# Attention, gated mixing and spatial gating on one core: how the probability-times-value products are queued, when the last weight chunks are read, and how fast the mixing is fed in

## The chip, the cores and the metric

The kernel runs on one core of one Trainium2 chip. The metric is the device time of one execution in microseconds. Three runs of the kernel before took 533.68, 536.41 and 536.85 us; the median, 536.41 us, is the time before. The engines are named as the profile names them: PE (TensorE, with PEld for its weight loads), DVE (VectorE), ACT (ScalarE), POOL (GpSimd), and SP, which issues most DMAs. Each engine works through its own list of instructions in order.

## The reference, cut to what matters

```python
# attention: B=4 batches, H=8 heads, S=576 positions, D=64
scores = q @ k.T / 8 + min(-(cum[:, None] - cum[None, :]), 0)   # causal, cum = cumsum(max(s, 0))
attn   = exp(scores - rowmax) / (rowsum + 1e-9)
x      = (attn @ v), heads side by side -> (B, 576, 512)
# gated mixing, then a spatial gate
gate = sigmoid(causal 5-tap convolution of x with conv_w)
y    = (gate * (x @ w_val)) @ w_out
h    = relu(y @ w_in);  u, v = halves of h
v_n  = (v - mean) / sqrt(var + 1e-6)
out  = (u * (w_spatial @ v_n + b_spatial)) @ w_out2
```

All of it is in fp32; where the kernel multiplies matrices of the mixing it splits each operand in a high and a low part and adds three products (`three`, L398 to L406).

## The kernel before, in words

The program is a Python function that emits instructions; a scheduler, which steps a model of the engines, then decides the order in which each engine's list holds them. What it is given is the order of emission, the dependencies, priorities, and here and there an order rule (`tc.issue_after(i)`: what is emitted inside the block stands behind instruction i). Nothing is looked at on the chip to choose the order: the lists are fixed.

**Attention, head by head.** The main loop (L674 to L713) steps over w = 0 to 32. At step w it computes the scores of head w in five query tiles (`scores`, L185): the scores' matmuls (L204 for the first eight heads, L206 and L207 after), a DVE reduction with the mask that gives the row's maximum (L214), and on ACT the exponential with its row sum (L219). It also transposes the probabilities of head w-1, 15 blocks of 128x128 in four banks, on PE (L266), and ACT copies each bank from PSUM to the tile `pt` (L267). Every second step it treats the finished pair of heads w-2 and w-1: the row sums are transposed on PE (`psr`, L234), copied by ACT (L236), written to DRAM by a DMA from ACT's queue (`r_d`, L237), and read back spread over the partitions by two DMAs from SP's queue (`R`, L243).

**The pair's products.** `pv` (L271) multiplies the transposed probabilities with v: 12 fp32 products for a pair, each of which is two MATMUL instructions on the chip. Head j = 0 writes PSUM partitions 0 to 63, head j = 1 partitions 64 to 127, so the two use the two halves of PE's columns. One group writes `psq` (the first 128 query positions: one 128-wide product per head), the other writes `pso` (the other 448 positions: widths 448, 448, 320, 192 and 64 per head). DVE then multiplies by `R` into the tile x (L289), and `conv` (L294) begins the convolution on ACT (L298) and goes on with four DVE steps (L301). In emission order each product is its own instruction with its own dependencies, so the scheduler may place each wherever the model has room. The first product of head j = 0 needs only that head's probabilities, which are there one step before those of head j = 1.

**Mixing, fed in between.** The mixing of a batch (`mixing_a`, L490, and `mixing_b`, L512) is a generator that yields after each group of 8 to 14 matmuls the time that the group is worth (1.44, 1.68 or 2.56). It is fed in five times per step by `more` (L606): a step adds `n_g` to an account, and groups are emitted until it is used up. `n_g` is 3 up to step 8, then 11.5, 10.0, 9.0 (steps 17 to 24) and 9.5 (steps 25 to 32). One batch is about 60 of these units. Batch b is queued at step 8(b+1)+1, the last batch behind the loop. The mixing's groups are what PE does while an attention step waits for ACT and DVE.

**The end.** Behind the loop (L714 to L718) `load_ahead` (L474) issues reads of weight chunks (512 KB each) for the third batch (`wo_d`) and the last batch (`wv_d`) into tiles that come free: `wv`, `pt`, `qk`, `cn`, `kd`. Then the last batch's `mixing_a` and `mixing_b` are emitted. `mixing_a` begins with xvh and xvl (L72, L79), the split of the four x tiles; its first matmuls (L404 to L406) need all four x tiles, so also the last pair's.

Of the kernel before, what the change touches and what calls it, by code (L numbers as in the profile page):

```python
# [24 lines left out]
def tile_stickbreak_attention_moe(  # L25
# [18 lines left out]
    NH, S = s.shape  # L44
    B = out.shape[0]
    H = NH // B
# [11 lines left out]
    BLK, w = {}, 0  # L58
# [5 lines left out]
    V, G, A, T, SY = nc.vector, nc.gpsimd, nc.scalar, nc.tensor, nc.sync  # L64
# [45 lines left out]
    cn = [early.tile([128, S], F32R, name=f"cn{i}") for i in range(2)]  # L110
    kds = [early.tile([128, S], F32R, name=f"kd{i}") for i in range(2)]
# [16 lines left out]
    r_d = dram.tile([NH // 2, 2, 5, 128], F32, name="r_d")  # L128
    wv_d = dram.tile([NP, 128, 2, 512], F32, name="wv_d")
    wo_d = dram.tile([NP, 128, 2, 512], F32, name="wo_d")  # L130
# [47 lines left out]
    LAST = {}  # L178
# [43 lines left out]
    R = {}  # L222
# [16 lines left out]
    def spread_sums(p):  # L239

        R[p] = early.tile([128, 5, 128], F32, tag="R", name="R", bufs=2)
        for j in range(2):
            SY.dma_start(R[p][64 * j:64 * j + 64].rearrange("p i q -> p (i q)"),  # L243
                         r_d[p, j].rearrange("i q -> (i q)").partition_broadcast(64))

    def evac_split(dst_hi, dst_lo, src):
        A.activation(dst_hi, src, AF.Copy)
# [23 lines left out]
    def pv(h):  # L271

        b, p = h // H, (h % H) // 2
        x = X[b, p] = early.tile([128, S], F32, tag=f"x{p}", name=f"x{p}", bufs=1)
        r = R.pop(h // 2).rearrange("p i q -> p (i q)")
        pts = [PT.pop(h + j) for j in range(2)]
        vs = [vraw.pop(h + j) for j in range(2)]
        for tag, q0, q1 in (("q", 0, 128), ("o", 128, S)):
            po = ps.tile([128, 512], F32, tag=tag, name=f"ps{tag}", bufs=1)
            cs = [c for c in range(5) if c * 128 < q1 and (c == 0 or q0 > 0)]  # L280
            for c in cs:
                a = max(q0, c * 128)
                o = BLK[c, c] + a - c * 128
                for j in range(2):
                    T.matmul(po[64 * j:64 * j + 64, a - q0:q1 - q0], vs[j][:, c, :], pts[j][:, o:o + q1 - a],  # L285
                             start=c == 0, stop=c == cs[-1])
            for a, e in ((q0, 64), (64, q1)) if q0 == 0 else ((q0, q1),):
                o = a + 64 if a else 0
                V.tensor_tensor(out=x[:, a:e], in0=po[:, a - q0:e - q0], in1=r[:, o:o + e - a], op=ALU.mult)  # L289
# [118 lines left out]
    KC = list(range(NP))  # L408
# [62 lines left out]
        key = src is wo_d, b, mc  # L471
        return AHEAD.pop(key) if key in AHEAD else load_chunk(src, mc)

    def load_ahead(src, b, homes):  # L474

        for mc, home in zip(KC, homes):
            AHEAD[src is wo_d, b, mc] = load_chunk(src, mc, home)

    def gated_split(dh, dl, psrc, other):
# [135 lines left out]
    def first_steps():  # L615
        nonlocal cw
        cw = early.tile([128, NP, 5], F32, name="cw")
        V.tensor_copy(cw, from_f64(conv_w, 20).rearrange("p (c k) -> p c k", k=5))
        order = [(lambda mc=mc: weight_prep(w_val, wv_d, mc)) for mc in KC]
        order += [(lambda mc=mc: fold_prep(mc, None)) for mc in KC]  # L620
        order = order[4:] + order[:4]
        for o in order:
            o()
            yield
        for kc in KC:
            fold_prep(kc, 1)
            yield
        for ec in range(4):
            fold(ec, 1)
            yield 2.56  # L630
# [14 lines left out]
    first = first_steps()  # L645
# [27 lines left out]
    for w in range(NH + 1):  # L673
        if w == H + 1:  # L674
            queue.clear()
            queue.append(start())
        elif w % H == 1 and w > 1 and w < NH:
            queue += [mixing_a(w // H - 1), mixing_b(w // H - 1)]
        if w >= NATIVE:
            load(w + 2)  # L680
        n_g = [3, 11.5, 10.0, 9.0, 9.5][0 if w <= H else 1 if w <= H + 4 else 2 if w <= 2 * H else 3 if w <= 3 * H else 4]
        gs = [n_g / 5] * 5
        if w < NH:
            scores(w, [0, 1])
        if w > 0:
            transposes(w - 1, [1, 2])
        if w % 2 == 0 and w > 0:
            lay_sums(w // 2 - 1)
        more(gs[0])
        if w < NH:  # L690
            scores(w, [2])
        prep(w + 1)
        if w > 0:
            transposes(w - 1, [3])
        more(gs[1])
        if w < NH:
            scores(w, [3])
        if w > 0:
            transposes(w - 1, [0])
        if w % 2 == 0 and w > 0:  # L700
            spread_sums(w // 2 - 1)
        more(gs[2])
        if w < NH:
            scores(w, [4])
            if w < NATIVE:
                load(w + 2)
            if w % 2:
                normalise(w // 2)
        more(gs[3])
        if w % 2 == 0 and w > 0:  # L710
            pv(w - 2)
            conv((w - 2) // H, ((w - 2) % H) // 2)
        more(gs[4])  # L713
    load_ahead(wo_d, B - 2, ["wv", "wv", "pt", "pt"])  # L714
    load_ahead(wv_d, B - 1, ["qk", "qk", cn, kds])
    queue += [mixing_a(B - 1), mixing_b(B - 1)]
    while queue:
        more(1)  # L718
# [50 lines left out]
```

## Time and profile before

| what | before |
|---|---|
| median of 3 runs | 536.41 us |
| profiled execution, its own time | 538.75 us |
| its span (first to last instruction) | 537.0 us |
| PE busy | 503.1 us, 94% of the span |
| ACT busy | 342.9 us, 64% |
| DVE busy | 314.0 us, 58% |
| POOL busy | 126.1 us, 23% |
| moved by DMA | 71.36 MB, mean 133 GB/s |
| mean granted TensorE clock | 0.981 |

The profile is one execution. In its views "busy" is the time in which an engine had an instruction, "x" the number of instructions, PEclk the granted clock of PE as a share of full speed (1.00 is the 2.4 GHz level, 0.50 the 1.2 GHz level). In a timeline, rows are instructions in order of time; equal neighbours are merged, and a bracket at the end is the idle time of the engine before the row with what ended it. Matmuls overlap: the duration of one is longer than the distance to the start of the next, so what a run of matmuls costs PE is read from start to start.

### The profile page before, as it was taken

What the parts mean: (1) busy time and instruction counts of PE and PEld (TensorE: products, weight loads), DVE (VectorE), ACT (ScalarE), POOL (GpSimd) and SP (SyncE); (2) the same over time, 40 slices, a digit from 0 to 9 for tenths busy, and PEclk for the clock granted to TensorE, in tenths of its full rate; (3) what the DMA queues carried; (4) which work ended last, traced back from release to release, by engine and by line L of the source; (5) the groups of instructions that cost most, each with busy time, mean ns of one, the idle gap of its engine ahead of it and who ended that gap; (6) DMA issues with size and microseconds to landing.
All of it is one profiled execution on the core that took longest, in us unless ns stands there. A gap on an engine that the chain in (4) does not pass through costs nothing.

```text
span 537.0 us, 9116 instructions
## 1 busy us (share of the span) xinstructions
PE 503.1 (94%) x3206; PEld 417.2 (78%) x3206; DVE 314.0 (58%) x836; ACT 342.9 (64%) x821; POOL 126.1 (23%) x166
## 2 busy tenths in 40 slices
PE   8777988999989999999999999999999999299997
PEld 4344655788768898988889898888789987298997
DVE  5778589788988865624886464565545541325120
ACT  3897679798678764954666475684867655234322
POOL 5220130016450112203351120032501300135240
PEclk9999889999999999999999999999999999689999
DMA  6949655437662633285331305763030178500002
GB/s 186 282 130 260 189 180 156 153 100 260 198 228 77 193 94 106 80 256 179 115 94 56 105 10 166 233 200 118 13 95 12 37 212 271 179 0 2 1 0 89
DMA packets 28910, 71.36 MB, mean 133 GB/s; under 512 B 4096, under 2 KB 12448, under 8 KB 28864
## 3 DMA queue, kind: packets, MB, share of 16 engines
q1 hardware_dynamic: 23936, 65.98, 40.6%
q10 hardware_dynamic: 4928, 4.80, 2.7%
q8 instruction: 25, 0.41, 0.3%
q14 instruction: 21, 0.17, 0.1%
HBM read 58.06 MB, written 9.16 MB: 125 GB/s over the span
## 4 chain that ended last, share of the span: by engine, by line
PE 64%; ACT 13%; DMA 12%; DVE 7%; issue 3%; SPq 1%; ACTq 0%; POOL 0%; DVEq 0%
PE psm L404 11%; PE psm L406 10%; PE psm L405 10%; PE pso L285 7%; PE pst L266 6%; PE psm L576 3%; PE psm L577 3%; PE psm L578 3%; ACT p L219 3%; DMA wg<-in_w_in 3%; PE pss L206 3%; DMA wr<-in_w_out 2%; PE pss L207 2%; ACT pt L267 2%; DMA R<-r_d 2%
## 5 line engine op out<-in xcount | busy, mean ns | idle before, releaser
L219 ACT ACTIVATE p<-p,nm 64x64 f32<-64x64 f32 (+4 forms) x160 | 88.6, 555 | 10.5 <-DVE nm L214 10.2
L266 PE MATMUL pst<-ident,p 128*128 128x128 f32 x480 | 77.6, 276 | 7.4 <-ACT pt L267 4.6
L214 DVE CUSTOM_DVE_ANT_0 p<-pss,mask 64x64 f32<-64x64 f32 (+4 forms) x160 | 64.3, 419 | 30.3 <-PE pss L207 19.2
L267 ACT ACTIVATE pt<-pst 128x512 f32<-128x512 f32 (+1 forms) x128 | 61.9, 494 | 21.8 <-PE pst L266 13.1
L266 PEld LDWEIGHTS pst<-ident,p 128*128 128x128 f32 x480 | 57.0, 141 | 22.8 <-ACT pt L267 8.2
L285 PE MATMUL pso<-pt,vraw 128*64 128x448 f32 (+3 forms) x320 | 66.1, 438 | 2.0 <-ACT pt L267 2.0
L301 DVE SCALAR_TENSOR_TENSOR z<-x,cw,z 128x575 f32<-128x575 f32 (+1 forms) x64 | 55.5, 867 | 6.9 <-ACT z L298 6.4
L79 POOL TENSOR_TENSOR g<-gt,g 128x288 fp32r<-128x288 f32 x32 | 28.5, 898 | 126.5 <-ACT g L72 126.5
L79 POOL TENSOR_TENSOR y<-gt,y 128x288 fp32r<-128x288 f32 x32 | 27.1, 845 | 108.9 <-ACT y L72 108.8
L206 PE MATMUL pss<-qk 128*64 128x64 f32 (+1 forms) x144 | 45.6, 333 | 1.1 <-DVE nm L214 1.1
L285 PEld LDWEIGHTS pso<-pt,vraw 128*64 128x64 f32 x320 | 28.4, 140 | 18.3 <-issue 8.7
L207 PE MATMUL pss<-kd,cn 66*64 66x64 f32 (+1 forms) x144 | 41.9, 296 | 0.0
L404 PE MATMUL psm<-g,wch 128*128 128x288 f32 x128 | 39.1, 306 | 0.0
L576 PE MATMUL psm<-wsh,vh 128*128 128x288 f32 x128 | 38.5, 303 | 0.0
L405 PE MATMUL psm<-g,wcl 128*128 128x288 f32 x128 | 37.8, 296 | 0.0
L406 PE MATMUL psm<-g,wch 128*128 128x288 f32 x128 | 37.7, 296 | 0.0
L577 PE MATMUL psm<-wsh,vl 128*128 128x288 f32 x128 | 37.5, 295 | 0.0
L578 PE MATMUL psm<-wsl,vh 128*128 128x288 f32 x128 | 37.5, 295 | 0.0
L404 PE MATMUL psm<-y,wv 128*128 128x288 f32 x112 | 34.3, 306 | 0.6 <-ACT pt L267 0.4
L481 DVE TENSOR_TENSOR gt<-psm,u 128x288 f32<-128x288 f32 x32 | 14.5, 454 | 34.7 <-PE psm L580 24.2
L406 PE MATMUL psm<-y,wv 128*128 128x288 f32 x112 | 33.1, 297 | 0.0
L405 PE MATMUL psm<-y,wv 128*128 128x288 f32 x112 | 32.9, 295 | 0.0
(171 smaller groups left out, 1310.9 us busy)
## 6 DMA issues: line engine op xcount, KB each, us to landing
raw<-in_qk SPq DMA_DIRECT2D x24, 576.0 KB
wv<-wo_d SPq DMA_DIRECT2D x16, 512.0 KB
wv<-wv_d SPq DMA_DIRECT2D x12, 512.0 KB
vraw<-in_vp SPq DMA_DIRECT2D x32, 160.0 KB
R<-r_d SPq DMA_DIRECT2D x32, 160.0 KB
out<-ot ACTq DMA_DIRECT2D x32, 144.0 KB
cn<-qk SPq DMA_DIRECT2D x24, 144.0 KB
wr<-in_w_in SPq DMA_DIRECT2D x5, 512.0 KB
```

The lines of the kernel that those rows point to most:

```text
L79: eng.tensor_tensor(out=out_, in0=in_, in1=f(hi), op=ALU.subtract)
L206: T.matmul(pst[0:m, o:o + b - a], qa[:, q0:q0 + m], kb[:, a:b], start=True, stop=False)
L214: LAST["V"] = V.tensor_tensor_reduce(out=p[i][0:m, a:b], in0=src, in1=mask[0:m, o:o + b - a], scale=-0.125, scalar=3.0e38 if a == 0 else n ...
L219: A.activation(p[i][0:m, 0:e], p[i][0:m, 0:e], AF.Exp, bias=nm[0:m, i:i + 1], scale=-1.0, accum_out=sm[h // 2 % 2][0:m, h % 2, i:i + 1])
L266: T.transpose(pt[:, o - o0:o - o0 + 128], p[i][:, c * 128:(c + 1) * 128], ident[:, r:r + 128])
L267: A.activation(PT[h][:, o0:end], pt[:, 0:end - o0], AF.Copy)
L285: T.matmul(po[64 * j:64 * j + 64, a - q0:q1 - q0], vs[j][:, c, :], pts[j][:, o:o + q1 - a], start=c == 0, stop=c == cs[-1])
L301: V.scalar_tensor_tensor(out=z[:, d:], in0=x[:, :S - d], scalar=cw[:, p, k:k + 1], in1=z[:, d:], op0=ALU.mult, op1=ALU.add)
L404: T.matmul(pt, ah, bh, start=j == 0, stop=False)
L405: T.matmul(pt, al, bh, start=False, stop=False)
L406: T.matmul(pt, ah, bl, start=False, stop=j == n - 1)
L576: T.matmul(o, vh[c][:, cs], wsh[:, c, hs[hf]], start=c == 0, stop=False)
```

## The change

Three edits:

1. In `pv` the pso group comes before the psq group, its first product is now that of block c = 1 of head j = 1, which reads the last bank that `transposes` fills, and every other product of the pair is emitted under `issue_after(first)`.
2. Behind the loop, only the first two `wo_d` chunks are issued freely. The other two and the four `wv_d` chunks are emitted under `issue_after` of the last `R` read.
3. `n_g` is 7.6 instead of 9.0 for steps 17 to 24 and 6.0 instead of 9.5 for steps 25 to 32.

```diff
-            SY.dma_start(R[p][64 * j:64 * j + 64].rearrange("p i q -> p (i q)"),
-                         r_d[p, j].rearrange("i q -> (i q)").partition_broadcast(64))
+            LAST["R"] = SY.dma_start(R[p][64 * j:64 * j + 64].rearrange("p i q -> p (i q)"),
+                                     r_d[p, j].rearrange("i q -> (i q)").partition_broadcast(64))
...
-        for tag, q0, q1 in (("q", 0, 128), ("o", 128, S)):
+
+        first = None
+        for tag, q0, q1 in (("o", 128, S), ("q", 0, 128)):
             po = ps.tile([128, 512], F32, tag=tag, name=f"ps{tag}", bufs=1)
-            cs = [c for c in range(5) if c * 128 < q1 and (c == 0 or q0 > 0)]
+            cs = [1, 0, 2, 3, 4] if q0 else [0]
             for c in cs:
                 a = max(q0, c * 128)
                 o = BLK[c, c] + a - c * 128
-                for j in range(2):
-                    T.matmul(po[64 * j:64 * j + 64, a - q0:q1 - q0], vs[j][:, c, :], pts[j][:, o:o + q1 - a],
-                             start=c == 0, stop=c == cs[-1])
+                for j in (1, 0):
+                    with ExitStack() as es:
+                        if first is not None:
+                            es.enter_context(tc.issue_after(first))
+                        m = T.matmul(po[64 * j:64 * j + 64, a - q0:q1 - q0], vs[j][:, c, :], pts[j][:, o:o + q1 - a],
+                                     start=c == cs[0], stop=c == cs[-1])
+                    first = first or m.ins
...
-    def load_ahead(src, b, homes):
+    def load_ahead(src, b, homes, mcs=KC):
-        for mc, home in zip(KC, homes):
+        for mc, home in zip(mcs, homes):
...
-        n_g = [3, 11.5, 10.0, 9.0, 9.5][0 if w <= H else 1 if w <= H + 4 else 2 if w <= 2 * H else 3 if w <= 3 * H else 4]
+        n_g = [3, 11.5, 10.0, 7.6, 6.0][0 if w <= H else 1 if w <= H + 4 else 2 if w <= 2 * H else 3 if w <= 3 * H else 4]
...
-    load_ahead(wo_d, B - 2, ["wv", "wv", "pt", "pt"])
-    load_ahead(wv_d, B - 1, ["qk", "qk", cn, kds])
+    load_ahead(wo_d, B - 2, ["wv", "wv"])
+    with tc.issue_after(LAST["R"].ins):
+        load_ahead(wo_d, B - 2, ["pt", "pt"], KC[2:])
+        load_ahead(wv_d, B - 1, ["qk", "qk", cn, kds])
```

What this does to the order shows best at three places. The first is PE's list around the eighth pair of heads, of 16. In the kernel before, its products stand in four pieces; here are the rows of the pieces with the row next to each (L207 is a scores matmul, L404, L576 and L580 are mixing matmuls, L266 a transposition; "x2" are two products of the same form):

```order
730 L207 MATMUL pss<-kd_99,cn_97 128x288
731 L285 MATMUL pso<-pt,vraw 64x448
732 L404 MATMUL psm<-g,wch 128x288
...
840 L285 MATMUL psq<-pt,vraw 64x128 x2
841 L285 MATMUL pso<-pt,vraw 64x448 x2
842 L266 MATMUL pst<-ident,p_106 128x128
...
870 L580 MATMUL psm<-ws_1735,s_137 128x288
871 L285 MATMUL pso<-pt,vraw 64x448
872 L285 MATMUL pso<-pt,vraw 64x320 x2
873 L285 MATMUL pso<-pt,vraw 64x192 x2
874 L285 MATMUL pso<-pt,vraw 64x64 x2
```

The same pair in PE's list of the changed kernel:

```order
824 L207 MATMUL pss<-kd_98,cn_96 128x288
825 L290 MATMUL pso<-pt,vraw 64x448 x4
826 L290 MATMUL pso<-pt,vraw 64x320 x2
827 L290 MATMUL pso<-pt,vraw 64x192 x2
828 L290 MATMUL pso<-pt,vraw 64x64 x2
829 L290 MATMUL psq<-pt,vraw 64x128 x2
830 L206 MATMUL pss<-qk 64x64
```

All 12 products now stand in one piece, head beside head, where before the first stood alone some 110 rows ahead. Of the 16 pairs, nine stand in one piece in the changed list; the second, third and fifth have the two psq products in a piece of their own; the ninth and the tenth have the last psq product alone, some 20 rows behind; the sixth is in three pieces; and in the eleventh each of the first four 448-wide products has a mixing matmul between it and the next. Only in the first and the fourteenth pair does the piece follow directly on a transposition.

The second place is SP's list at the end of the loop (R is the read of the spread row sums, the others are weight chunks). Before:

```order
187 L466 DMA wv<-wo_d 128x1024 x3
188 L466 DMA wqk<-wv_d 128x1024
189 L466 DMA wv<-wo_d 128x1024
190 L462 DMA cn_97<-wv_d 128x512
191 L462 DMA kd_99<-wv_d 128x512
192 L466 DMA wv<-wo_d 128x1024 x2
193 L466 DMA wpt<-wo_d 128x1024 x2
194 L243 DMA R<-r_d 64x640 x2
195 L466 DMA wpt<-wo_d 128x1024 x2
```

And in the changed kernel:

```order
186 L243 DMA R<-r_d 64x640 x4
187 L472 DMA wqk<-wv_d 128x1024 x2
188 L468 DMA cn_96<-wv_d 128x512
189 L468 DMA cn_97<-wv_d 128x512
190 L468 DMA kd_98<-wv_d 128x512
191 L468 DMA kd_99<-wv_d 128x512
192 L472 DMA wpt<-wo_d 128x1024 x2
193 L472 DMA wv<-wo_d 128x1024 x2
194 L472 DMA wpt<-wo_d 128x1024 x2
```

The last pair's two reads of R stood behind all but two of the late chunks and now stand ahead of all of these. The changed list also holds four `wo_d` reads fewer (16 instead of 20): before, the third batch's `mixing_b` had already read its own chunks when `load_ahead` read them again.

The third place is PE's list behind the last pair's products. Before, the next rows are the rest of the last batch's first two groups, which read the last pair's x. In the changed list 166 mixing matmuls of the third batch stand between (70 of the spatial stage, L582 to L586, and 96 of the last product, which read y), and only then the last batch begins; this is where it does:

```order
2341 L410 MATMUL psm<-y,wpt 128x288
2342 L411 MATMUL psm<-y,wpt 128x288
2343 L412 MATMUL psm<-y,wpt 128x288
2344 L410 MATMUL psm<-xvh_5150,wqk 128x288
2345 L411 MATMUL psm<-xvh_5150,wqk 128x288
```

Before, 18 of the last batch's matmuls stood ahead of the last pair's products; now none does.

## Rows read from the trace of the kernel before

**Rows 1.** The page, part 1: busy time of each engine
```profile
PE 503.1 (94%) x3206; PEld 417.2 (78%) x3206; DVE 314.0 (58%) x836; ACT 342.9 (64%) x821; POOL 126.1 (23%) x166
```

**Rows 2.** Windows: stretch, its length, busy time per engine, clock, DMA share
```profile
core 0: us, PE busy (x) PEld busy (x) DVE busy (x) ACT busy (x) POOL busy (x), PEclk, DMA share, GB/s
0.00:100.00 100.00, 83.94 (x403) 51.87 (x404) 75.02 (x223) 74.01 (x193) 22.82 (x39) 0.97 0.67 196
100.00:180.00 80.00, 77.55 (x466) 62.16 (x465) 66.85 (x167) 65.78 (x150) 25.05 (x28) 1.00 0.53 165
180.00:445.00 265.00, 263.62 (x1830) 230.68 (x1829) 149.84 (x401) 173.47 (x420) 56.07 (x69) 1.00 0.39 119
445.00:456.00 11.00, 10.26 (x75) 8.13 (x73) 1.38 (x6) 5.43 (x12) 0.00 (x0) 1.00 0.90 313
456.00:465.00 9.00, 0.01 (x1) 0.01 (x1) 1.49 (x4) 1.35 (x2) 0.00 (x0) 0.70 0.85 269
465.00:473.10 8.10, 7.01 (x28) 6.66 (x29) 4.34 (x8) 3.19 (x5) 2.68 (x3) 0.50 0.00 2
```

**Rows 3.** Windows of line L285 alone: length, PE busy, PEld busy, clock, DMA
```profile
0.00:100.00 100.00, 19.75 (x96) 9.10 (x96) 0.97 0.67 196
100.00:180.00 80.00, 10.81 (x58) 4.22 (x58) 1.00 0.53 165
180.00:445.00 265.00, 37.36 (x206) 16.11 (x206) 1.00 0.39 119
```

**Rows 4.** Timeline of PE around the eighth pair: start, duration, line, operation, tiles
```profile
188.24 0.29 PE L207 MATMUL pss<-kd,cn 66*128 66x288 f32 x1
188.46 0.97 PE L285 MATMUL pso<-pt,vraw 128*64 128x448 f32 x2
189.36 0.40 PE L404 MATMUL psm<-g,wch 128*128 128x288 f32 x1
...
203.78 0.44 PE L285 MATMUL psq<-pt,vraw 128*64 128x128 f32 x4
204.05 0.92 PE L285 MATMUL pso<-pt,vraw 128*64 128x448 f32 x4
...
208.90 1.94 PE L285 MATMUL pso<-pt,vraw 128*64 128x448 f32 x14
```

**Rows 5.** Timeline of PE at the last pair and behind it
```profile
446.74 0.30 PE L405 MATMUL psm<-y,wv 128*128 128x288 f32 x1
446.88 0.29 PE L406 MATMUL psm<-y,wv 128*128 128x288 f32 x1
...
452.34 0.97 PE L285 MATMUL pso<-pt,vraw 128*64 128x448 f32 x4
...
453.36 1.89 PE L285 MATMUL pso<-pt,vraw 128*64 128x448 f32 x14
464.99 0.61 PE L404 MATMUL psm<-xvh,wqk 128*128 128x288 f32 x1 [9.74 <-ACT xvh L72]
465.40 0.44 PE L405 MATMUL psm<-xvh,wqk 128*128 128x288 f32 x1
465.64 0.44 PE L404 MATMUL psm<-xvh,wqk 128*128 128x288 f32 x1
...
467.89 0.61 PE L404 MATMUL psm<-xvh,wqk 128*128 128x288 f32 x1 [1.09 <-DVE gt L481]
```

**Rows 6.** The chain that ended last: row sums of two pairs, start and duration
```profile
94.79 1.93 DMA r_d<-rt
...
97.26 3.85 DMA R<-r_d
...
451.52 4.82 DMA r_d<-rt
456.86 5.69 DMA R<-r_d
```

**Rows 7.** The page, part 5: ACT's copies of transposed banks
```profile
L267 ACT ACTIVATE pt<-pst 128x512 f32<-128x512 f32 (+1 forms) x128 | 61.9, 494 | 21.8 <-PE pst L266 13.1
```

## The prediction

> **What bounds the kernel now.** First the page's busy times: PE is busy 503.1 of 537.0 us, no other engine above 64% [rows 1]. A share over the whole span mixes stages, so next the windows [rows 2]. From 180 to 445 us PE is busy 263.62 of 265 us at full clock while ACT is busy 65% and DVE 57%: here PE is the limit, and every microsecond of PE work removed is a microsecond, as long as no wait replaces it. From 0 to 100 us PE is busy 84%, ACT 74%, DVE 75%, and the DMA share is 0.67: a chain through several engines. From 100 to 180 us PE is busy 97%, but DVE 84% and ACT 82%: PE work removed there may surface on the others. Then 456 to 465 us: nothing runs on PE at all, and from 465 to 473.1 us it runs at granted clock 0.50, the 1.2 GHz level, after that idle time.
>
> Two things are to be seen below these totals. In the timeline around a pair [rows 4], the first 448-wide product stands alone: two MATMULs that hold PE from 188.46 to 189.36, 0.90 us. At 452.34 four such MATMULs, one product of each head, take 0.97 us, just what the two take alone (0.97) [rows 4, 5]: the two heads' products run side by side in the two halves of the columns, so a product without its partner wastes half of PE. In the timeline behind the last pair [rows 5], PE waits 9.74 us for the last batch's xvh. The chain says why [rows 6]: the last pair's row sums took 4.82 us to DRAM and 5.69 us back, where an earlier pair's took 1.93 and 3.85; the DMA share was 0.90 and 0.85 around them [rows 2], which is the late chunks.
>
> **The change, part by part**, against the profiled execution's 538.75 us.
>
> *The end.* In the changed order 166 mixing matmuls stand between the last pair's products and the first that needs its x. Warm, one follows the other at 0.134 us (446.74 to 446.88) [rows 5], so they cover 22 us. What they must cover: before, with slow transfers, the wait was 9.74 us. So the gap goes even if the transfers stay slow, and with the chunks behind R they should fall towards 1.93 and 3.85 us. The next wait, 1.09 us at 467.89 for DVE's gating behind the convolution, is under the same cover. The half clock goes with the gap that preceded it: 7.01 busy us at a distance of 0.24 us (465.40 to 465.64) instead of 0.134 [rows 2, 5] cost 7.01 x (1 - 0.134/0.24) = 3.1 us. Together 9.74 + 1.09 + 3.1 = 13.9 us. What is late next are the chunks themselves: two `wo_d` chunks in `pt` are needed 118 matmuls (15.8 us) behind the pair, and 2 MB of `wv_d` plus 1 MB of `wo_d` must land by then or 22 us. At the 313 GB/s of the stretch 445 to 456 us [rows 2], 3 MB take 10 us. They fit, with 6 us to spare; the four repeated reads that are gone make it easier.
>
> *The pairs, 180 to 445 us.* Line L285 is busy 37.36 us for 206 MATMULs [rows 3]; a pair has 24, so this is 8.6 pairs at 4.35 us each. The price of one piece can be read: in the last pair 11 of 12 products stand together, from 452.34 to 453.36 + 1.89 = 455.25, 2.91 us [rows 5], and the twelfth fits beside them, since head 1 with all six of its products is the longer side already. Saved per pair 4.35 - 2.91 = 1.44 us, times 8.6 = 12.4 us; the last pair adds its lone product, 0.90 us (the same form as at 188.46). Against that, three pairs of the changed order are not whole: two have a lone psq product (about 0.45 us each, an estimate: the two 128-wide products at 203.78 hold PE 0.27 us before the next group, and a piece of its own costs an entry and an exit), and the eleventh has four lone 448s, 4 x 0.90 = 3.6 instead of at most 2 x 0.97 us side by side, with its entries 2.0 us more. Net 12.4 + 0.9 - 2.9 = 10.4 us. Each entry into a piece costs PE 0.22 us after a 288-wide matmul instead of 0.134 (188.24 to 188.46) [rows 4]; three fewer per pair would be 2 us more. I leave that out, since busy time counts the overlap of a piece's last MATMUL with the next row, which is about as much.
>
> *The pairs, 0 to 180 us.* From 100 to 180 us 58 MATMULs take 10.81 us [rows 3]: 2.4 pairs at 4.47, so at most 3.8 us. DVE and ACT are over 80% busy there; between nothing and all I take half, 1.9. From 0 to 100 us, four pairs take 19.75 us, waits and half clock included; at most 4 x 1.5 = 6 us. PE is not the limit there; I take a quarter, 1.5.
>
> *The slower feeding.* No work is removed: 1.4 and 3.5 units per step move behind the attention, where PE has nothing else, so this costs nothing by itself and fills the gap above. Its price is cover. In steps 25 to 32 a step loses 3.5 units, 3.9 us of PE's work at 12 matmuls of 0.134 us for 1.44. What may come bare: ACT's convolution start waits for x, x for R, and the exponentials of the next head queue behind it on ACT. With 1.93 + 3.85 us and some 0.5 us of issue [rows 6], R lands 6.3 us behind the row sums' copy. In the changed order these four pairs' products begin 36 to 57 rows behind the row sums' transposition, 5 to 8 us, and take 2.9. So from 0 (R lands first) to 6.3 us for each of four pairs, 25 us. The stretch from 180 to 445 us, where PE idles 1.4 of 265 us with the same chain in it [rows 2], is nearest: I take 2.5 us.
>
> Sum: 538.75 - 13.9 - 10.4 - 1.9 - 1.5 + 2.5 = 513.6. The median of before is 2.3 us below its profiled execution, so 511.2 as the median of runs.
>
> On thinning there is a rule that speaks against it. At 180 to 445 us, with transpositions mixed in, the clock was 1.00; at 0 to 100 us, where feeding is 3 units a step, it was 0.97 [rows 2]. The Trainium skill ("TensorE: Matmul & The Clock Gate", Part 4, PE-mode transpose) states that transposes do not count as PE-busy in the way other matmuls do, so a stage with less mixing could lose the clock. By the trace's rows at 1.00 the sum stays 511.2; by that rule it would be the third rival below.
>
> **The rivals.**
> - *The pairs give nothing*: ACT and DVE or the heads' chain set the steps once PE is faster. For it: 82 to 84% busy before 180 us. Against it: 57 to 65% after, and PE waits of 1.4 us. Only the end is gained: 536.4 - 13.9 = 522.5.
> - *All of it arrives*: no new waits, and the pairs bring 10.4 + 3.8 + 6 = 20.2, since x comes sooner from whole pieces and the steps before 180 us shorten with them: 536.4 - 13.9 - 20.2 = 502.3. Against it: PE's 84% before 100 us.
> - *The thinned stage behaves like the opening*: PE busy 84%, clock 0.97 [rows 2]. A step before took 265 / 17.2 heads = 15.4 us; less 3.9 and half of 1.44 it is 10.8, eight of them 86 us. 16% of that is 14 us of waits, and 3% is 3 us of clock: 511.2 + 17 = 528. Against it: ACT had weights to convert in the opening, and none here.
> - *Slower*: each piece waits at the head of PE's list for ACT to copy the last bank, with everything behind it held. It decides from (25.2 + 5.4)/16 = 1.9 us a pair, the whole gain and 1% more. An ACT copy is 0.49 us [rows 7], so it would take two or three other ACT instructions ahead of it each time. In the changed order only 2 of 16 pieces follow directly on a transposition, so it should stay at a microsecond or two in all; if it held for every pair at 2.5 us, 551 (511.2 + 40).
>
> **How the numbers follow.** Chances: the forecast (505 to 518) 0.62, all of it (about 502) 0.13, nothing from the pairs (about 522) 0.13, the opening's behaviour (about 528) 0.08, slower 0.04. The predicted time is the forecast's, 511. The range 502 to 523 takes in the bounds of the pairs' saving and leaves out the last two cases and half of the second, near 2 in 10. A measurement of this kernel can tell about 1%, so faster is below 531.0: 0.62 + 0.13 + 0.13 and the faster edge of the fourth, 0.89; within 1% 0.07; slower 0.04.
>
> **What would show it.** Right: no PE wait over 2 us before the last batch's first matmul and granted clock 1.00 from 440 us on; L290 at about 3 us per pair; the last r_d and R near 2 and 4 us; 2 MB less moved. Wrong: PE busy below 95% in steps 25 to 32, with DVE's x waiting for R or ACT's z for x ahead of exponentials; a PE wait for `wpt` behind the last pair; a granted clock of 0.50 in that stage; pairs at 3 us with the stage no shorter.

## The result and the profile after

| what | before | after |
|---|---|---|
| median | 536.6 us (4 runs) | 523.4 us (522.2 to 524.2, 4 runs) |
| ratio after/before | | 0.975, interval 0.972 to 0.979 |
| profiled execution, its span | 538.75, 537.0 us | 524.15, 522.4 us |
| moved by DMA | 71.36 MB | 69.27 MB |
| mean granted clock | 0.981 | 0.967 |

The change is a gain of 13.3 us in the medians. The prediction was 511.0 us with a range of 502 to 523, so it had the sign, but the gain came out about half as large: the time lies 0.4 us above the range. That it lies near the rival in which the pairs give nothing (522.5) is chance, as the terms below show.

The page's busy times of after, then its windows by the stretches of [rows 2] (stretch, its length, busy time of each engine, granted clock, DMA share; the end is cut otherwise, since the gap is gone):

```profile
PE 493.0 (94%) x3206; PEld 414.2 (79%) x3206; DVE 316.6 (61%) x836; ACT 339.9 (65%) x819; POOL 125.1 (24%) x166
0.00:100.00 100.00, 86.52 (x406) 54.35 (x408) 78.45 (x227) 76.11 (x195) 22.47 (x39) 0.90 0.64 197
100.00:180.00 80.00, 73.73 (x441) 58.90 (x438) 62.32 (x159) 60.30 (x140) 23.87 (x28) 0.94 0.51 156
180.00:340.00 160.00, 158.05 (x1143) 140.96 (x1143) 101.05 (x265) 107.62 (x269) 33.58 (x40) 1.00 0.42 129
340.00:430.00 90.00, 86.94 (x616) 75.97 (x615) 49.88 (x143) 66.74 (x154) 18.39 (x25) 0.98 0.40 122
430.00:480.00 50.00, 48.69 (x319) 45.32 (x318) 17.98 (x34) 17.01 (x36) 17.31 (x24) 1.00 0.27 85
```

The end is as forecast: 48.69 of 50 us busy at clock 1.00, where before had a hole and half clock [rows 2]. The opening is worse than in [rows 2]: the clock is 0.90 for 0.97 up to 100 us, and from 100 to 180 us PE is busy 73.73 us at 0.94 where it was 77.55 at 1.00. From 180 to 430 us PE now stands still 5.0 of 250 us, before 1.4 of 265.

The windows of the pair products' line, now L290 (length, PE busy, PEld busy, clock), and the timeline of PE at the eighth and the eleventh pair (start, duration, line, tiles, equal neighbours merged):

```profile
180.00:430.00 250.00, 32.44 (x240) 15.18 (x240) 0.99 0.41 126
...
205.94 2.70 PE L290 MATMUL pso<-pt,vraw 128*64 128x448 f32 x20
208.47 0.39 PE L290 MATMUL psq<-pt,vraw 128*64 128x128 f32 x4
...
296.36 0.96 PE L290 MATMUL pso<-pt,vraw 128*64 128x448 f32 x2
297.26 0.40 PE L412 MATMUL psm<-g,wch 128*128 128x288 f32 x1
297.59 0.96 PE L290 MATMUL pso<-pt,vraw 128*64 128x448 f32 x2
298.48 0.40 PE L410 MATMUL psm<-g,wch 128*128 128x288 f32 x1
```

A whole pair takes 2.92 us (205.94 to 208.86), where the prediction had 2.91, and ten pairs take 3.24 each for 4.35 in [rows 3]. The eleventh, and in part three others, are not whole: mixing matmuls stand between the products.

In the waits of PE (what it waited for; us in total, times, the longest), 0 to 180 us, first before, then after:

```profile
PE pst L266 <- ACT pt L267: 4.6, 6, 1.2
PE pso L285 <- ACT pt L267: 2.0, 3, 1.2
...
PE pst L266 <- ACT pt L267: 8.2, 10, 2.9
PE pso L290 <- ACT pt L267: 2.9, 3, 2.2
```

PE waits 11.1 us for ACT's copies in the opening, before 6.6.

**Where the 25.2 us of the forecast went.** I counted PE's time behind 180 us in both traces from the start of each matmul to the start of the next; time in which PE is idle is a term of its own. The matmuls other than the pair products are counted at the warm median of their form. What lies above it is an entry, where a pair product comes next, or half clock, where the granted clock was 0.50, or the rest.

| term | forecast | measured |
|---|---|---|
| opening: more left to do at 180 us (other matmuls 294.6 to 296.6, and ten more of the pairs' MATMULs, 1.3) | -3.4 | +3.4 |
| pair products behind 180 us, for the same number (38.8 to 30.0), and entries into them (3.3 to 1.9) | -10.4 | -10.2 |
| gap ahead of the last batch | -9.7 | -9.7 |
| half clock behind 180 us (3.5 at the end to none; none to 1.4 at 394 us) | -3.1 | -2.1 |
| other idle time of PE behind 180 us (2.5 to 6.3) | -1.1 + 2.5 | +3.9 |
| rest (1.5 to 1.4) | | -0.2 |
| sum | -25.2 | -14.9 (spans: -14.6) |

The two terms named outright, pairs and end, came as forecast. 6.8 us were lost in the opening and 2.5 in idle time behind it. Some 2 us or more of the opening need not be the change's: the first pair ends at 42.0 us instead of 39.9, behind half clock from 12.1 to 22.3 us, where PE's order was still the same; kernels with the old opening show that half clock too.

### The profile page after: what moved, and what is told of

It is laid out like the page before. It is cut to its first block, busy times and chain, and to the rows that moved or that the text cites. A ratio compares the mean times of both kernels' runs of the same rounds, so it can differ in the third digit from the quotient of the medians.

```text
span 522.4 us, 9111 instructions
## 1 busy us (share of the span) xinstructions
PE 493.0 (94%) x3206; PEld 414.2 (79%) x3206; DVE 316.6 (61%) x836; ACT 339.9 (65%) x819; POOL 125.1 (24%) x166
## 2 busy tenths in 40 slices
DMA packets 28334, 69.27 MB, mean 133 GB/s; under 512 B 4032, under 2 KB 12384, under 8 KB 28288
## 4 chain that ended last, share of the span: by engine, by line
PE 44%; ACT 4%; DVE 3%; DMA 2%; issue 1%; POOL 1%; ACTq 0%; POOLq 0%
PE psm L410 9%; PE psm L412 8%; PE psm L411 8%; PE pso L290 4%; PE pst L266 4%; DMA out<-ot 2%; PE psm L582 2%; PE psm L583 2%; PE psm L584 2%; DVE z L307 2%; PE pss L206 1%; PE pss L207 1%; ACT L219 1%; PE psm L586 1%; PE psm L585 1%
## 5 line engine op out<-in xcount | busy, mean ns | idle before, releaser
L266 PE MATMUL pst<-ident,p 128*128 128x128 f32 x480 | 81.7, 286 | 11.0 <-ACT pt L267 9.1
L266 PEld LDWEIGHTS pst<-ident,p 128*128 128x128 f32 x480 | 60.0, 146 | 24.3 <-ACT pt L267 13.6
L290 PE MATMUL pso<-pt,vraw 128*64 128x448 f32 (+3 forms) x320 | 50.5, 449 | 2.9 <-ACT pt L267 2.9
L290 PEld LDWEIGHTS pso<-pt,vraw 128*64 128x64 f32 x320 | 22.9, 145 | 30.6 <-issue 19.8
L207 PE MATMUL pss<-kd,cn 66*64 66x64 f32 (+1 forms) x144 | 42.0, 298 | 0.0
L582 PE MATMUL psm<-wsh,vh 128*128 128x288 f32 x128 | 38.2, 302 | 0.6 <-DVE gt L487 0.6
L487 DVE TENSOR_TENSOR gt<-psm,z 128x288 f32<-128x288 f32 x32 | 14.3, 452 | 32.8 <-PE psm L412 31.6
L72 ACT ACTIVATE qk<-raw 128x576 fp32r<-128x576 f32 x48 | 30.2, 676 | 4.4 <-PE pss L206 4.3
L379 POOL TENSOR_TENSOR wa<-wr 128x512 int32<-128x512 int32 x12 | 13.9, 1162 | 77.1 <-DVE wr L375 26.9
```

The source lines that it names most:

```text
L266: T.transpose(pt[:, o - o0:o - o0 + 128], p[i][:, c * 128:(c + 1) * 128], ident[:, r:r + 128])
L290: m = T.matmul(po[64 * j:64 * j + 64, a - q0:q1 - q0], vs[j][:, c, :], pts[j][:, o:o + q1 - a], start=c == cs[0], stop=c == cs[-1])
L582: T.matmul(o, vh[c][:, cs], wsh[:, c, hs[hf]], start=c == 0, stop=False)
```

## The experiments

Ratios are against the kernel before on the same chip; the changed kernel's is 0.975.

| kernel | opening (pairs 1 to 5) | pairs 6 to 16 | last pace | median us | ratio, interval |
|---|---|---|---|---|---|
| e1 | new | rule | 9.5, late chunks free | 531.3 | 0.993 (0.990 to 0.996) |
| e2 | old | old | 6.0 | 541.2 | 1.009 (1.006 to 1.012) |
| e3 | old | rule | 6.0 | 521.8 | 0.973 (0.969 to 0.977) |
| e5 | new | rule | 7.5 | 537.0 | 1.003 (1.000 to 1.006) |
| e8 | new | whole | 6.0 | 526.8 | 0.981 (0.977 to 0.985) |
| e9 | old | whole | 6.0 | 511.5 | 0.953 (0.950 to 0.957) |
| e10 | new | whole | 7.5 | 521.0 | 0.971 (0.967 to 0.975) |
| e11 | new | whole | 9.5 | 528.1 | 0.984 (0.979 to 0.988) |
| e12 | old, 5th whole | whole | 6.0 | 515.0 | 0.962 (0.959 to 0.965) |
| e13 | 1 to 4 whole, 5th old | whole | 6.0 | 523.4 | 0.977 (0.974 to 0.980) |
| e14 | old | whole | 7.5 | 515.0 | 0.962 (0.957 to 0.968) |
| e15 | new order, no rule | whole | 6.0 | 526.1 | 0.983 (0.980 to 0.986) |
| e16 | old, 4th whole | whole | 6.0 | 519.2 | 0.968 (0.962 to 0.975) |
| e17 | 1 to 3 whole, 4th and 5th old | whole | 6.0 | 519.7 | 0.969 (0.963 to 0.975) |
| e18 | old | whole | 9.5 | 512.5 | 0.955 (0.950 to 0.961) |
| e19 | old | whole | 6.0, late chunks free | 510.3 | 0.953 (0.945 to 0.961) |
| e20 | old | whole | 9.5, late chunks free | 511.6 | 0.956 (0.953 to 0.959) |
| e21 | old | old, with precedence | 9.5, late chunks free | 536.4 | 1.001 (0.998 to 1.003) |

"New" and "rule" are the changed kernel's products behind their last part; "whole" adds precedence over the mixing (in e8, e10 and e11 the first five pairs have it too; in e8 this changes nothing in PE's order up to 110 us). The pace 9.5 stands for the old pair of 9.0 and 9.5; the others go with the changed 7.6. The kernels of this table were measured in five groups, each beside the kernel before, whose median was 535.2 to 537.4 us; a difference of 2 us between kernels of different groups is not told apart.

### First: the parts of the change

Theory A: the loss lies in the opening. Theory B: it lies in the slower feeding.

**e1**, the pieces alone (before with the changed `pv`).

> The kernel before with the pair products in one piece and nothing else. Theory A (the pieces save about 10 us from 180 us on, but cost some 7 to 10 us up to 125 us, where PE is waited for less and drops to half clock): the end gap of 9 to 10 us stays, so 536.6 - 10 + 8 = about 534. Theory B (the pieces give some 13 us everywhere and what is missing went in the slower feeding): about 523.

531.3, between the two and nearer theory A's 534. The gap at the end is still there, as this row of PE's waits from 425 us on shows, against 9.74 in [rows 5]:

```profile
PE psm L410 <- ACT xvh L72: 9.3, 1, 9.3
```

**e2**, the end alone (after, with the old `pv`):

```
-            cs = [1, 0, 2, 3, 4] if q0 else [0]        # and the rule
+            cs = [c for c in range(5) if c * 128 < q1 and (c == 0 or q0 > 0)]
```

> The changed kernel with the products of before: slower feeding and late chunks alone. PE's order is that of before up to step 17, so the opening is that of before. Theory A: the whole end gain less a little, 536.6 - 13.9 + 2.5 = about 525. Theory B (slower feeding costs about 10 us of bare waits in steps 25 to 32): about 533.

541.2, slower than before, although the gap is gone: no wait above 0.5 us from 425 us on. The windows of its pair products against [rows 3], then PE's timeline inside one pair:

```profile
180.00:445.00 265.00, 50.69 (x216) 18.20 (x216) 0.99 0.37 113
...
360.44 0.96 PE L285 MATMUL pso<-pt,vraw 128*64 128x448 f32 x2
361.66 0.75 PE L285 MATMUL pso<-pt,vraw 128*64 128x320 f32 x2
```

A pair costs 50.69 x 24/216 = 5.63 us, before 4.35: the slower pace breaks the pairs into lone products. Counted behind 180 us as above, against before: products +9.5, entries +4.9, other matmuls left to do +1.2, other idle time +0.8, half clock -1.9, rest -0.2, and the gap's 9.7 off, together +4.6 us. Neither theory had this.

**e3**, the first five pairs as before, the rest as in after; **e5**, after with another pace:

```
+    def pv(h):
+        (pv_old if h < 10 else pv_new)(h)                       # e3
-        n_g = [3, 11.5, 10.0, 7.6, 6.0][...]
+        n_g = [3, 11.5, 10.0, 7.6, 7.5][...]                    # e5
```

> The changed kernel, but the first five pairs' products are emitted as before; PE's order is that of before for the first 470 of its 2953 rows (about 125 us), with the mixing that before had there. Theory A (the loss lies in the opening): 523.4 - 9 = about 514, granted clock in the opening as before (0.97). Theory B: the first five pairs' pieces gain rather than lose, 523 to 526.

> The changed kernel with 7.5 instead of 6.0 units per step in steps 25 to 32; PE's order is the changed kernel's for its first 1769 rows. 12 units fewer remain behind the attention, about 8 of the 20, so some 9 us cover the last pair's 10 to 15 us. Theory A (thinning cost only 3 to 5 us): 521 to 525. Theory B: 517 or less.

e3 took 521.8, hardly less than after; e5 took 537.0, 14 us more. The windows of the pair products, of e3, of after for the same stretch, and of e5:

```profile
180.00:340.00 160.00, 21.81 (x120) 8.78 (x120) 1.00 0.40 121
...
180.00:340.00 160.00, 20.75 (x144) 9.33 (x144) 1.00 0.42 129
...
340.00:465.00 125.00, 20.29 (x96) 7.47 (x96) 0.99 0.38 116
```

In e3 the five pairs from 180 to 340 us cost 4.36 us each, where six cost 3.46 each in after; these 4.5 us hide a part of what the old opening gave. In e5 the last four cost 5.07. The rule keeps the other products behind the first, but does not keep mixing matmuls out from between them. A and B both fall: the parts act on each other through the order in which products and mixing are interleaved.

### Second: whole pairs (theory C) at three paces

```
                             es.enter_context(tc.issue_after(first))
+                        es.enter_context(tc.high_priority(offset=1000))
                         m = T.matmul(po[...], vs[j][:, c, :], pts[j][...])
```

This puts a pair's products ahead of ready mixing matmuls in PE's list, so that each pair from the 6th on is one block. e8 is after with it, e9 is e3 with it, e10 is e5 with it, e11 is after at the old pace with it.

> The changed kernel, with the 24 products of a pair given precedence over the mixing groups in the order, so that each pair from the 6th on stands in PE's list as one block (in the changed kernel the 6th, 9th, 10th and 11th are split, and cost 3.2, 3.2, 3.2 and 4.9 us where whole ones cost 2.85). Theory C (the loss against the forecast lies in split pieces and in the opening): the pieces give 0.3 + 0.4 + 0.4 + 2.1 = 3.2 us, the opening stays as it is: 520 us. Theory D (a split costs nothing in the end, since PE then waits elsewhere): 523 us, as the changed kernel.

> The same precedence, and the first five pairs queued as before the change. Theory C: the kernel with the old opening alone took 521.8 us, with 10th and 11th pairs of 6.24 and 5.05 us; whole they cost 2.85 each, 5.6 us less: 516 us, and 514 if the waits around the split pairs go too. Theory D: 522 us. In both the 500th mixing product should come near 215 to 220 us, as with the old opening, and not at 227 as in the changed kernel.

> The changed kernel with the last pace 7.5 instead of 6.0, and the same precedence. With the pace of 7.5 alone the time was 537.0 us, and its 13th, 15th and 16th pairs were split (6.67, 4.80 and 4.22 us). Theory C: the 14 us lost by 7.5 came from the splits and the waits beside them; whole pairs give 3.8 + 1.95 + 1.4 + 2.1 = 9.3 us back, and the waits (2.25 and 1.91) too: 524 us, within 4 us of the whole kernel at 6.0. Theory E (the pace itself costs, since work for the last batch's PE is used up sooner): 533 us or more.

> The changed kernel with the old pace (9.0 and 9.5), and the same precedence. Theory C: the pieces are whole at any pace, so what the pace is worth is only the gap at the end, 9.3 us in the kernel with the pieces alone and its half clock: 531 us, and 528 if the late chunks shorten it. Theory F (with whole pairs the pace doesn't matter, the gap was due to the splits): 522 us.

e10 goes C's way: 537.0 became 521.0, 3 us below its number. e9 gained 10.3 us over e3 and came 2.5 below C's 514; that it lies 0.5 us from the forecast for the change is chance, since it is another kernel. But e8 is 3.4 us slower than after, where C said 3 faster. In the profiles its products take some 3 us less behind 180 us, but PE is busy 154.27 us from 180 to 340 us, in after 158.05: there the saving came back as waits, as theory D had it. e11 has C's number (528), but not its reason: there is no gap, only a wait of 4.3 us for weight chunks, and it lies 1.3 us from e8, which is F's reading of the pace. The windows of e9, for comparison with those of after, and of its pair products (L311):

```profile
0.00:100.00 100.00, 90.13 (x417) 55.93 (x418) 76.53 (x227) 75.84 (x195) 23.35 (x39) 0.91 0.68 203
100.00:180.00 80.00, 78.59 (x495) 65.53 (x495) 68.80 (x175) 67.65 (x159) 28.86 (x29) 1.00 0.51 168
...
180.00:420.00 240.00, 26.93 (x228) 13.54 (x224) 1.00 0.42 129
```

The products cost 26.93 x 24/228 = 2.83 us a pair. And with the old opening PE is busy 168.7 of the first 180 us, in after 160.3. In before it was 161.5 [rows 2], with the same order on every engine up to 110 us: so e9's lead is not the old opening's alone, and busy time counts half clock as work. In warm time of the other matmuls, before had done 114.9 us by 180 us, after 112.9, e9 120.0. Opening and whole pairs bring 11.9 us together, and apart 1.6 (e3) and -3.4 (e8): these are not terms that add.

### Third and fourth: which pairs of the opening

```
-        (pv_old if h < 10 else pv_new)(h)
+        (pv_old if h < 8 else pv_new)(h)                    # e12: 5th whole
+        (pv_old if h == 8 else pv_new)(h)                   # e13: 1 to 4 whole
+        (pv_old if h < 10 and h != 6 else pv_new)(h)        # e16: 4th whole
+        (pv_old if 6 <= h < 10 else pv_new)(h)              # e17: 1 to 3 whole
```

e15 has in the first five pairs the new order of the parts, without rule and precedence; e14 is e9 at pace 7.5.

> As the fastest kernel so far (511.5 us: first five pairs queued as before the change, the rest as whole blocks), but the 5th pair too as a whole block. Theory G (the opening's loss is made by the 5th pair: as a block it stands behind ACT's last copy of it, at 118.9 us in the changed kernel, while both buffers of the mixing are full until the gate): 518 to 524 us, and the 100th mixing product near 127 us instead of 116. Theory H (it is made by the first four: the 4th pair's x is 2.5 to 4.5 us later, and so are the first sigmoid and the gate): 512 to 514 us, the 100th mixing product at 116 to 118.

> As the kernel of 511.5 us, but of the first five pairs only the 5th is queued as before the change; the first four are queued as blocks. Theory G: 511 to 514 us, the sigmoid of the first batch may be late but the 100th mixing product stays at 116 to 119 us. Theory H: 519 to 525 us, the sigmoid at 115 us as in the changed kernel (109 in the kernel of 511.5), the 100th mixing product near 127.

> As the kernel of 511.5 us, with the last pace 7.5 instead of 6.0. Theory C (once pairs are whole, a pace between the old one and 6.0 costs nothing at the end, since the last pair still comes before the mixing runs out, and it fills PE better in the last quarter): 506 us, as 7.5 brought 5.8 us with whole pairs and the new opening (526.8 to 521.0). Theory E (7.5 uses up the mixing work before the last pair is done): 515 us or more, with a wait of PE of over 2 us just ahead of the last batch's first product.

> As the kernel of 511.5 us, but the first five pairs have the new order of their parts (the part of the last copy first, psq behind pso) without the rule that holds the other products behind the first. If the rule makes the opening's loss: 511 to 514 us. If the order of the parts does (pso, the larger, ahead of psq, and the late part first): 520 to 526 us, as the kernel with the rule and whole pairs (526.8).

e12 515.0, e13 523.4: the first four pairs make the loss (theory H), the 5th adds 3.4. e15 at 526.1 says that the order of the parts is enough for it, without the rule. e14 at 515.0 has theory E's number, but not its sign: no gain from the pace, and no wait of PE over 0.5 us from 400 to 450 us.

> As the kernel of 511.5 us (first five pairs as before the change, the rest whole blocks), with the 4th pair too as a block. Theory H1 (the opening's loss comes through the 4th pair alone: its x, late, delays the batch's first sigmoid and so the gate for which the mixing waits): 519 to 523 us, nearly as with the first four as blocks (523.4), sigmoid at 113 us. Theory H2 (each block takes filler from a PE that waits in the opening, a quarter of the 11.9 us for each pair): 514.5 us, sigmoid at 109 to 110.

> As the kernel of 511.5 us, with the first three pairs as blocks and the 4th and 5th as before the change. Theory H1: 511 to 514 us. Theory H2 (three quarters of 11.9 us, or more since PE waits most in 0 to 75 us): 519 to 523 us, PE busy below 41 us in the stretch 25 to 75 (45.3 in the kernel of 511.5, 39.5 in the changed kernel).

e17 (519.7) is H2's number. PE's waits from 0 to 180 us in e9, then in e17, and the window 25 to 75 us of both in the same order:

```profile
PE pst L266 <- ACT pt L267: 2.0, 4, 0.8
PE pso L285 <- ACT pt L267: 1.4, 2, 1.2
...
PE pst L266 <- ACT pt L267: 7.6, 8, 2.3
PE pso L311 <- ACT pt L267: 1.9, 2, 1.4
...
25.00:75.00 50.00, 45.29 (x233) 27.26 (x233) 40.63 (x126) 43.11 (x113) 10.55 (x8) 0.97 0.70 211
25.00:75.00 50.00, 38.80 (x212) 23.28 (x212) 43.43 (x130) 43.35 (x114) 10.80 (x9) 0.97 0.67 207
```

As blocks, the products no longer fill the waits of PE for ACT's copies: 9.5 us of such waits for 3.4, and 6.5 us less busy between 25 and 75 us at the same clock. That is most of e17's 8.2 us.

e16 (519.2) is near H1's number, but not by H1's way: its first batch's sigmoid on ACT started at 102.4 us, earlier than e9's 110.2, and its 100th mixing matmul at 112.5 for 116.3. It was level with e9 at the 300th (172.0 for 171.6), 2.4 us behind at the 1100th and 7.0 at the 1300th (417.7 for 410.7), so it lost its lead between 139 and 172 us. Most of its time, 5.1 us, it lost between 380 and 396 us: PE is busy 2.47 of 4.4 us up to 385.8, and then the granted clock is 0.50 up to 392.6. What brings these waits about, with the 4th pair as a block, I have not found.

### Fifth: is the pace needed, are the late chunks?

e18 is e9 at the old pace; e19 is e9 without the rule on the late chunks (SP's list alone differs); e20 has neither, so it is before with whole blocks from the 6th pair; e21 is before with the precedence alone.

```
-        n_g = [3, 11.5, 10.0, 7.6, 6.0][...]
+        n_g = [3, 11.5, 10.0, 9.0, 9.5][...]                # e18, e20
-    with tc.issue_after(LAST["R"].ins):                     # e19, e20
```

> As the kernel of 511.5 us, with the old pace (9.0 and 9.5). My prediction's end term (13.9 us for gap, wait and half clock, less 2.5 for slower feeding) gives 511.5 + 11.4 = 523 us, and a gap of PE of 7 us or more ahead of the last batch's first product. If the slower feeding costs more than I took (528.1 against 526.8 us with the new opening says that it costs nearly what the gap gives): 513 to 517 us, with the gap still there.

> As the kernel of 511.5 us, but the last batch's chunks of the weights are no longer held behind the last read of row sums: SP's list alone differs, PE's, ACT's and DVE's are the same. By the prediction (the rule takes out the wait of 1.09 us and lets the last x start early): about 1 to 3 us slower, 512.5 to 514.5. If the pace has made the rule idle: 511.5, with the last read of row sums at the same distance behind its write.

> The kernel before with one edit: from the 6th pair on, a pair is a whole block with precedence over the mixing; first five pairs, pace and late chunks as before. Theory J (whole blocks bring the last pair forward by themselves, so neither pace nor late chunks are needed): 511 to 514 us, as the kernel of 512.5 with the late chunks held back, and no wait of PE for ACT's xvh before the last batch. Theory K (the late chunks must be held back when the pace is the old one): 515 us or more, with that wait back.

> The kernel before with the products of the pairs from the 6th on given precedence over the mixing, but in their old order and without the rule, so that each goes as soon as its copy is there: the pairs stay split in parts of 1, 2, 2 and 7 products. If the precedence alone moves the last pair ahead of the gap: 520 to 525 us. If it takes the blocks: 531 to 537, since the last pair's last product keeps its place in PE's list and a pair still costs about 4 us.

e18 512.5, e19 510.3, e20 511.6, e9 511.5, their intervals one over the other: with the old opening and whole pairs neither the pace nor the order of the late chunks does anything that these runs can tell. My own end term said 523 for e18, for e20 theory J said 511 to 514, which came, and theory K 515 or more. The rows at the end of e20: the last pair's block, ACT's last xvh, the first matmul of the last batch; behind them PE's first matmul of the last batch in before, and e21's wait:

```profile
435.30 2.70 PE L311 MATMUL pso<-pt,vraw 128*64 128x448 f32 x20
439.65 0.67 ACT L72 ACTIVATE xvh<-x 128x576 fp32r<-128x576 f32 x1
441.43 0.29 PE L434 MATMUL psm<-xvh,wqk 128*128 128x288 f32 x1
...
448.45 0.38 PE L404 MATMUL psm<-xvh,wqk 128*128 128x288 f32 x1
...
PE psm L407 <- ACT xvh L72: 7.4, 1, 7.4
```

In before the last batch began at 448.45, ahead of the last pair's last eleven products at 452.34 [rows 5]; in e20 at the old pace it begins at 441.43, behind the last pair, whose xvh is ready 1.1 us ahead. There is no gap and no wait over 0.9 us. e21 shows that precedence without the block does not do this: its pairs cost 4.3 us as before (37.26 us for 208 MATMULs), the wait is 7.4 us, the time that of before.

**A better kernel.** e20, one edit on the kernel before, and e19 are 4.4 to 4.7% faster than before and some 12 us faster than the changed kernel.

## Why the prediction failed, point by point

- **The pairs' price: right.** 2.91 us forecast for a whole pair, 2.92 measured; 10.4 us forecast behind 180 us, 10.2 measured. That the eleventh would be split was read from the order and came (four lone products, its pieces hold PE 4.93 us).
- **The end: right, but not the only way to it.** Gap and half clock at the end went, 12.8 us forecast and 13.2 counted; the wait of 1.1 us was replaced by others of 1.3 us. Within the change it is the pace that removed the gap: e1, without it, keeps 9.3 us, and e2, with it, has none. But e20 has no gap at the old pace either: what makes the gap is that the last pair's products stand behind the last batch's first in PE's list, and whole blocks with precedence move them ahead by themselves.
- **The pairs from 0 to 180 us: the step that failed.** I bounded it by "nothing" on one side and all on the other and took 3.4 us of gain; 3.4 us of loss were measured. No row excluded a loss. The reading behind it, that work on an engine which is not the limit costs little wherever it stands, missed what those lone products did: they filled PE's waits for ACT. As blocks behind the last copy they leave the waits bare (6.6 to 11.1 us in after, 3.4 to 9.5 between e9 and e17). With whole pairs from the sixth on, the first four pairs as blocks cost 11.9 us (e13 against e9), the 5th 3.4. The profiles agree: by 180 us the nine kernels with at least the first three pairs in the new order had done 111.8 to 114.0 us of the other matmuls' warm time, the eight with these as before and the new order from the sixth pair on 118.5 to 121.4, and before 114.9. So the term took as one two parts of opposite sign: the first pairs lose as blocks, and from the sixth on they gain already ahead of 180 us. Only for the first three is the loss traced to the waits for ACT; for the 4th (e16) the cause stays open.
- **Slower feeding: near its size, but waits that the pieces bring were put at nothing.** 2.5 us were forecast. PE's other idle time behind 180 us rose by 3.9 us, and 1.4 us of half clock came. The windows of before, then of e1, which has the pieces at the old pace:

```profile
180.00:340.00 160.00, 159.33 (x1117) 139.56 (x1116) 93.49 (x250) 100.59 (x251) 33.01 (x39) 1.00 0.41 127
340.00:430.00 90.00, 89.29 (x604) 77.51 (x602) 50.60 (x138) 63.91 (x148) 23.07 (x30) 1.00 0.31 90
...
180.00:340.00 160.00, 157.22 (x1158) 142.20 (x1157) 97.03 (x260) 105.14 (x266) 34.60 (x40) 1.00 0.43 133
340.00:430.00 90.00, 89.04 (x626) 78.83 (x624) 48.59 (x138) 64.69 (x148) 23.50 (x30) 1.00 0.33 101
```

From 340 to 430 us, where the pace is 6.0, after idles 3.1 us, before 0.7 and e1 1.0: some 2 us go with the pace, near the forecast. From 180 to 340 us after idles 2.0 us, before 0.7, but e1 2.8: these waits are there without the slower pace, so they go with the pieces, for which I had taken none. With the old opening and whole pairs the pace makes no difference (e18). What I had not considered is that pace sets how the order interleaves products and mixing: the same pace without the rule broke the pairs to 5.63 us (e2), and a pace between with the rule broke the last four to 5.07 (e5).

- **Additivity.** The sum took pieces and pace as terms of their own. Pieces alone gave 4.7 us (e1), pace and late chunks alone cost 5 (e2), the two together gave 13.3.
- **Late chunks: no measurable part** in e19, with the old opening; in the changed kernel itself the rule was not tried alone. That 2 MB less are moved was right. The last row sums were quick: R was issued 1.27 us behind r_d, before 4.84; in e20, without the rule, 1.6.
- **The rivals.** The time came out at the first rival's (522.5), but not by its way: behind 180 us the pairs, and the end, gave all they were to give. The third rival's sign did show: granted clock 0.50 from 394.4 to 397.8 us in the thinned stage, worth 1.4 us, behind 4.4 us in which PE was busy for 2.27. Two windows of after, then the window from 340 to 430 us of e9 and of e20:

```profile
390.00:394.40 4.40, 2.27 (x14) 1.56 (x12) 1.82 (x7) 4.36 (x7) 0.79 (x2) 1.00 0.01 1
394.40:397.80 3.40, 3.40 (x13) 3.08 (x14) 2.93 (x10) 3.38 (x8) 2.08 (x3) 0.50 0.03 7
...
340.00:430.00 90.00, 87.80 (x629) 77.04 (x627) 54.73 (x135) 61.52 (x144) 23.69 (x30) 1.00 0.35 110
340.00:430.00 90.00, 87.05 (x615) 78.35 (x614) 49.31 (x134) 62.17 (x145) 24.30 (x30) 0.98 0.32 96
```

e9, with the same pace and the same transpositions, held 1.00 here; e20, at the old pace, fell to 0.50 from 391.8 to 395.3 us, behind 4.4 us in which PE was busy for 2.25. So in after and e20 the fall comes behind waits, and it doesn't need the thinning. What the Trainium skill ("TensorE: Matmul & The Clock Gate", Part 4, PE-mode transpose) says of transposes may bear on all of them alike; these runs don't separate it. The slower rival did not come: PE waited 2.2 us for a block's last copy once, at 118.9 us (in the waits of after above, L290), and in no later pair for long. The waits that came in the opening are mostly those of the transpositions (4.6 to 8.2 us), and no rival had them.

## What to carry to other kernels

A product that is sent early and alone may cost twice its price on a busy engine and still be worth it where that engine waits: make blocks where the engine is the limit, and leave the pieces loose in a stage in which it waits for another. A rule that keeps instructions behind one of them doesn't keep others from coming between; look in the new order for how many pieces each block has, at each setting of a pace that goes with it, before giving the block its whole saving. And where two edits meet in one queue's order, a sum of their separate gains is no forecast: the pair of edits is one term, with a range as wide as both.

## What the runs showed of the hardware

In before, e3 and e9 the order is the same on every engine up to 110 us, and the granted clock is not: it was 0.50 from 9.5 to 23.1 us in e9, from 15.7 to 22.6 in e3, and in before not until 53.5 us, but then up to 56.9 and again from 70.5 to 73.9. The first pair ended at 39.9 us in before, 40.0 in e3 and 42.5 in e9; PE's 261st MATMUL began at 73.9, 69.7 and 70.9 us. So 2 to 4 us of an opening can differ between two profiles without any edit, which is as much as some terms of the sum above.
